# Storing the last 128 tokens of an attention and SwiGLU kernel in output order

## The chip, the cores and the metric

The kernel runs on one core of a Trainium2 chip. The metric is the time of one execution in device microseconds (us); lower is better. A core has five engines that run side by side and signal each other with semaphores: TensorE (PE: matmuls, with the loading of weights, PEld, beside them), VectorE (DVE), ScalarE (ACT), GpSimd (POOL) and SyncE (SP). Transfers between DRAM and the on-chip memory (SBUF) are issued by SP, ACT or POOL and carried out by 16 DMA engines. Matmuls write to PSUM, which has eight banks.

## The reference

Inputs are `q`, `k`, `v` of shape (8, 8, 576, 64), that is batch, head, token and head dimension, and three weight matrices. Linear attention gives 8 x 576 = 4608 rows of 512, and a SwiGLU block works on these:

```python
q_s = softmax(q, axis=-1)                 # over the head dimension
k_s = softmax(k, axis=2)                  # over the tokens
kv  = einsum('bhsd,bhse->bhde', k_s, v)
a   = einsum('bhsd,bhde->bhse', q_s, kv)
x   = a.transpose(0, 2, 1, 3).reshape(4608, 512)
g   = x @ w_gate                          # 512 -> 1536
out = (g * sigmoid(g) * (x @ w_val)) @ w_out   # 1536 -> 512, float32
```

## The kernel before

**Token order.** A batch has S = 576 tokens. Token number 9p + t of a batch (p from 0 to 63, t from 0 to 8; T = 9) is loaded so that a partition holds nine neighbouring tokens. In the transposed activations `xt` the column of that token is 576b + 64t + p. So 64 neighbouring columns are 64 tokens that lie nine rows apart in the output, and a block of 128 columns is two such groups, t and t + 1.

**Stages.** Attention of a batch (exponentials on ACT, sums and normalization on DVE, transposes, small matmuls) fills `xt`. The feed-forward part runs over chunks of columns: the first has 576, the second 448, and seven more have 512. The function `m_unit` (line 272) makes one of 12 slices of the hidden layer for a chunk: 4 matmuls for the gate and 4 for the value (line 284), a Silu on ACT (line 291) into `sg`, and one multiply on DVE (line 292) into `hr`. `hr` is a ring of 1536 columns. The function `o_unit` (line 320) then multiplies 128 columns of `hr`, as the stationary operand, with `wo` (12 matmuls, line 309), copies the 128 x 512 result to SBUF (line 110) and stores it with `store` (line 294). Because hidden columns become output partitions, the partition order of the result is the column order of `hr`. So `store` needs two transfers, each from 64 partitions to rows that lie nine apart.

**Order.** All instructions are written out by hand inside `tc.manual_schedule()`. The output blocks of one chunk are made among the units of the next (lines 524 to 547). In the last chunk (`final`, columns 4096 to 4607), units stand beside the output blocks 28 to 30; behind the units come block 31 (line 556), blocks 32 to 34 of the last chunk itself, and block 35 with `o_last` (line 323). `o_last` makes the 512 output columns in two pieces, 320 and 192, each with 12 matmuls (line 329), a copy (line 333) and a store of its own, so that the first piece is stored while the second is computed.

**Queues.** All output blocks but the last are stored by SP, two issues each. The last block's two pieces are stored by SP (lower 64 partitions) and ACT (upper 64). SP also issues the loads of `q`, `k`, `v` (line 77) and the DMA transposes (line 180), in program order. `load_kv(b)` (line 83) loads keys and values of batch b for both groups G of four heads; it is called for batches 4 to 7 in unit 8 of the chunk two batches earlier. The loads of the last batch are cut in two pieces (`BANKS`: t from 0 to 4, and 5 to 8), all but the values of G = 1. The transfers of SP and ACT take eight completion semaphores in turn, and a transfer waits until the one before it on the same semaphore has landed.

Of the kernel before, what the change touches and what calls it, by code (L numbers as in the profile page):

```python
# [15 lines left out]
def kernel(  # L16
# [10 lines left out]
    nc = tc.nc  # L27

    B, H, S, D = q.shape
    d_model, d_ff = moe_w_gate.shape  # L30
# [3 lines left out]
    T = S // 64  # L34
# [3 lines left out]
    BANKS = ((0, 5), (5, T))  # L38
# [8 lines left out]
    def bank(name):  # L47
        return psp.tile([128, 512], FP32, tag="ps", name=name)
# [5 lines left out]
    hr = const.tile([128, MT, RING], BF16, name="hr", tag="hr")  # L54
# [10 lines left out]
    def head_ap(src, b, G, t0=0, t1=T):  # L65
        return bass.AP(
            tensor=src.tensor,
            offset=src[b, 4 * G].offset + 64 * t0,
            ap=[[T * 64, 128], [2 * HSTR, 2], [1, (t1 - t0) * 64]],
        )  # L70

    def load(what, src, b, G, pieces=((0, T),), after=None):
        t_ = ld.tile([128, 2, T * 64], FP32, tag=what, name=what)
        raw[what, b, G] = t_
        last = None
        for t0, t1 in pieces:
            last = nc.sync.dma_start(out=t_[:, :, 64 * t0:64 * t1], in_=head_ap(src, b, G, t0, t1))  # L77
            if after is not None:
                tc.add_manual_dep(last.ins, after.ins.name, SYNC, reason="order of loads")
                after = None  # L80
        return last

    def load_kv(b):
        whole = ((0, T),)
        last = b == B - 1
        for G in range(NG):
            load("k", k, b, G, BANKS if last else whole)
            load("v", v, b, G, BANKS if last and G == 0 else whole)

    def w_slice(dst, src, c0, n):  # L90
        ap = bass.AP(
# [24 lines left out]
    def exp_of(what, b, G, pieces=((0, T),)):  # L116
        s = st.setdefault((b, G), {})
        e = s["e" + what] = at.tile([128, T, 2, 64], BF16, tag="e" + what, name="e" + what)
        src = raw[what, b, G].rearrange("p h (t d) -> p t h d", d=64)
        for t0, t1 in pieces:  # L120
            nc.scalar.activation(out=e[:, t0:t1], in_=src[:, t0:t1], func=AF.Exp)  # L121
# [21 lines left out]
    def norm_mul(b, G, pieces=((0, T),), engs=None):  # L143
        s = st[b, G]
        eq2 = s["eq"].rearrange("p t h d -> p (t h) d")
        qs = s["qs"] = at.tile([128, T, 128], BF16, tag="qs", name="qs")
        for (t0, t1), eng in zip(pieces, engs or (nc.vector, nc.vector)):
            n = 2 * (t1 - t0)
            last = eng.tensor_mul(  # L149
                qs[:, t0:t1, :].rearrange("p t (h d) -> p (t h) d", d=64),  # L150
                eq2[:, 2 * t0:2 * t1, :],
                s["rr"][:, 2 * t0:2 * t1].to_broadcast([128, n, 64]),
            )
        return last
# [22 lines left out]
    def turn_dma(b, G):  # L177
        s = st[b, G]
        qt = s["qt"] = at.tile([128, T, 128], BF16, tag="qt", name="qt")
        nc.sync.dma_start_transpose(out=qt, in_=s["qs"].rearrange("p t c -> p (t c)"))  # L180
# [38 lines left out]
    def kv_both(b):  # L219
        if ("kv", b) not in st:  # L220
            st["kv", b] = [bank("kv") for _ in range(2)]
        for G in range(NG):
            kv_mm(b, G, st["kv", b], 256 * G)

    def scale_both(b):
        kn = st["kn", b] = at.tile([128, 2, NG, 64], BF16, tag="kn2", name="kn2")
        for g in range(2):
            kv = st["kv", b][g].rearrange("p (G c) -> p G c", c=256)
            kvr = at.tile([128, NG], FP32, tag=f"kvrr{g}", name="kvr")
            nc.vector.reciprocal(out=kvr, in_=kv[:, :, 64])  # L230
            nc.vector.tensor_mul(kn[:, g], kv[:, :, 0:64], kvr.to_broadcast([128, NG, 64]))
# [37 lines left out]

    def m_unit(c0, n, m, by_group=False):
        ms = slice(m * 128, (m + 1) * 128)
        parts = [(c0, n)] if n <= 512 else [(c0, 320), (c0 + 320, n - 320)]
        gu = []
        for nm in ("g_ps", "u_ps"):
            ps = [bank(nm) for _ in parts]
            gu.append(ps)
        steps = [(a, kk, i) for a in range(2) for kk in range(KT) for i in range(len(parts))]
        if by_group:  # L280
            steps.sort(key=lambda a: (a[1] // 2, a[0], a[2], a[1]))
        for a, kk, i in steps:
            c, w_ = parts[i]
            nc.tensor.matmul(  # L284
                out=gu[a][i][:, 0:w_], lhsT=(wg, wv)[a][:, kk, ms], rhs=xt[:, kk, c:c + w_],
                start=(kk == 0), stop=(kk == KT - 1),
            )
        for g_ps, u_ps, (c, w_) in zip(gu[0], gu[1], parts):
            r = c % RING
            sg = ff.tile([128, 512], BF16, tag="sg", name="sg")  # L290
            nc.scalar.activation(out=sg[:, 0:w_], in_=g_ps[:, 0:w_], func=AF.Silu)  # L291
            nc.vector.tensor_mul(hr[:, m, r:r + w_], sg[:, 0:w_], u_ps[:, 0:w_])  # L292

    def store(j, o_sb, c0=0, c1=512, engs=(nc.sync, nc.sync)):
        for half in range(2):
            b, t = divmod(2 * j + half, T)
            dst = bass.AP(
                tensor=out.tensor,
                offset=out[b * S + t, c0].offset,
                ap=[[T * d_model, 64], [1, c1 - c0]],  # L300
            )
            engs[half].dma_start(out=dst, in_=o_sb[64 * half:64 * half + 64, c0:c1])

    def o_mm(j, o_ps=None, m0=0, m1=MT):
        if o_ps is None:
# [14 lines left out]
    def o_unit(j):  # L320
        o_out(j, o_mm(j))

    def o_last(j):
        r0 = (j * 128) % RING
        o_sb = osb.tile([128, 512], FP32, tag="o_sb", name="o_sb")
        for c0, n in ((0, 320), (320, 192)):
            o_ps = bank("o_ps")
            for m in range(MT):
                nc.tensor.matmul(  # L329
                    out=o_ps[:, 0:n], lhsT=hr[:, m, r0:r0 + 128], rhs=wo[:, m, c0:c0 + n],  # L330
                    start=(m == 0), stop=(m == MT - 1),
                )
            nc.vector.tensor_copy(out=o_sb[:, c0:c0 + n], in_=o_ps[:, 0:n])  # L333
            store(j, o_sb, c0, c0 + n, (nc.sync, nc.scalar))

# [1 line left out]
    with tc.manual_schedule():  # L339
# [113 lines left out]
        for m in range(MT):  # L453
            m_unit(0, S, m, by_group=(m == 0))
# [6 lines left out]
        p = [None, None]  # L461
# [43 lines left out]
        for ci, (c0, n) in enumerate(chunks):  # L505
            b = ci + 2
            jo = 4 * ci
            att = b < B
            more = b + 1 < B
            final = ci == len(chunks) - 1  # L510
            for m in range(MT):
                if ci == 0:
                    if m == 3:
                        norm_mul(b, 1)
                        turn_dma(b, 1)
                    elif m == 5:
                        kv_both(b)
                        scale_both(b)
                    elif m == 6:
                        exp_of("k", b + 1, 0)  # L520
                        exp_of("k", b + 1, 1)
                        cast_v(b + 1, 0)
                        cast_v(b + 1, 1)
                elif m == 3:
                    if att:
                        exp_of("q", b, 0)
                        exp_of("q", b, 1)
                        norm_sum(b, 0)
                    o_unit(jo)
                    if att:  # L530
                        norm_mul(b, 0)
                        turn_dma(b, 0)
                    o_unit(jo + 1)
                    if att:
                        norm_sum(b, 1)
                elif m == 4 and att:
                    norm_mul(b, 1)
                    turn_dma(b, 1)
                elif m == 7:
                    if more:  # L540
                        exp_of("k", b + 1, 0)
                        exp_of("k", b + 1, 1)
                        cast_v(b + 1, 0)
                        cast_v(b + 1, 1)
                    o_unit(jo + 2)
                    if not final:
                        o_unit(jo + 3)
                if m == 8 and more:
                    for G in range(NG):
                        load("q", q, b + 1, G)  # L550
                    if b + 2 < B:
                        load_kv(b + 2)
                m_unit(c0, n, m, by_group=(ci == 0 and m == 0))
                if att and m == (10 if ci == 0 else 9):
                    x_and_next_kv(b)
        o_unit(jo + 3)
        last = n_tok // 128 - 4
# [33 lines left out]
```

## Time and profile before

| what | value |
|---|---|
| median of 4 runs | 312.23 us (312.04 to 312.9) |
| the profiled execution's own time | 312.04 us |
| its span, first to last instruction | 309.8 us |
| granted TensorE clock | 0.998 of full |
| TensorE busy | 301.5 us, 97% of the span |
| DVE, ACT, POOL busy | 160.7, 146.2 and 32.8 us |
| last matmul of the last block ends, by the chain | 305.9 us |
| last copy to SBUF | 305.94 to 306.30 us |

A page gives the busy time of each engine and the chain of work that ended last, followed back from the last instruction. A row of a group has the line, the engine, the operation, output and input names, shapes and the count, then the busy time and the mean of one in ns, then the engine's idle time before these instructions and what ended it. Timeline rows begin with the start and the duration in us; "x2" merges neighbours. Issue rows have the count, the KB of one transfer and the us from issue to landing. SPq and ACTq are the queues of SP and ACT.

### The profile page before, as it was taken

How to read it: one execution, taken by the hardware profiler on the slowest of the kernel's cores; microseconds unless marked ns; L12 is line 12 of the kernel's file. 1: busy time of each engine (PE TensorE's matmuls, PEld its weight loads, DVE VectorE, ACT ScalarE, POOL GpSimd, SP SyncE). 2: the span in 40 equal slices, each digit the busy share in tenths (PEclk: the TensorE clock that was granted, in tenths of full speed). 3: DMA queues.
4: the chain of work that ended last, by engine and by line, in shares of the span. 5: the costliest groups of instructions: out<-in, count | busy, mean ns of one | idle time of the engine just before them, and what ended most of it. 6: DMA issues, size and time to landing. Idle time of an engine off the chain costs nothing.

```text
span 309.8 us, 5455 instructions
## 1 busy us (share of the span) xinstructions
PE 301.5 (97%) x2182; PEld 149.7 (48%) x2182; DVE 160.7 (52%) x274; ACT 146.2 (47%) x214; POOL 32.8 (11%) x39
## 2 busy tenths in 40 slices
PE   6799999999999999999999999999999999999995
PEld 2588745554444444454444444444444444444443
DVE  3844487945754566365826493539353324333321
ACT  5743578785674375447464737455043113312300
POOL 2960021510200110002000200000000000000000
PEclk9999999999999999999999999999999999999999
DMA  7999999999337815590739252505310302020034
GB/s 271 192 197 207 277 389 390 352 209 389 90 76 218 310 34 111 138 381 11 144 75 362 92 123 62 182 0 107 73 34 0 70 13 55 3 68 11 22 70 104
DMA packets 42506, 45.78 MB, mean 148 GB/s; under 512 B 19568, under 2 KB 27248, under 8 KB 42480
## 3 DMA queue, kind: packets, MB, share of 16 engines
q1 hardware_dynamic: 33568, 39.99, 43.3%
q0 software_dynamic: 8752, 5.31, 12.0%
q8 instruction: 17, 0.28, 0.3%
q10 hardware_dynamic: 160, 0.13, 0.2%
q14 instruction: 9, 0.07, 0.1%
HBM read 37.75 MB, written 9.44 MB: 152 GB/s over the span
## 4 chain that ended last, share of the span: by engine, by line
PE 94%; DMA 2%; DVE 1%; ACT 0%; SPq 0%; issue 0%
PE g_ps L284 30%; PE u_ps L284 30%; PE o_ps L309 29%; DMA q<-in_q_dram 2%; PE kv L189 2%; PE xp L245 1%; PE o_ps L329 1%; PE tp L164 0%; DVE qs L149 0%; DVE rs L135 0%; SPq L77 0%; PE xp L202 0%; ACT eq L121 0%; ACT xt L259 0%; DVE o_sb L333 0%
## 5 line engine op out<-in xcount | busy, mean ns | idle before, releaser
L291 ACT ACTIVATE sg<-g_ps 128x512 bf16<-128x512 f32 (+2 forms) x120 | 64.6, 554 | 133.6 <-PE g_ps L284 131.8
L292 DVE TENSOR_TENSOR hr<-sg,u_ps 128x512 bf16<-128x512 bf16 (+2 forms) x120 | 74.2, 630 | 87.3 <-PE u_ps L284 81.6
L284 PE MATMUL g_ps<-xt,wg 128*128 128x512 bf16 (+2 forms) x480 | 111.4, 358 | 0.1
L284 PE MATMUL u_ps<-xt,wv 128*128 128x512 bf16 (+2 forms) x480 | 111.3, 358 | 0.0
L309 PE MATMUL o_ps<-wo,hr 128*128 128x512 bf16 x420 | 93.9, 379 | 0.0
L284 PEld LDWEIGHTS <-wv 128*128 128x128 bf16 x480 | 47.0, 98 | 46.4
L284 PEld LDWEIGHTS <-wg 128*128 128x128 bf16 x480 | 46.3, 98 | 45.5 <-issue 0.6
L309 PEld LDWEIGHTS <-hr 128*128 128x128 bf16 x420 | 40.9, 98 | 48.6
L110 DVE COPY o_sb<-o_ps 128x512 f32<-128x512 f32 x33 | 22.5, 680 | 39.2 <-PE o_ps L309 39.2
L124 POOL CAST vb<-v 128x1152 bf16<-128x1152 f32 x14 | 17.9, 1281 | 136.1 <-DMA v<-in_v_dram 128.6
L135 DVE TENSOR_REDUCE rs<-eq 128x18 f32<-128x1152 bf16 (+2 forms) x18 | 21.7, 1214 | 13.1 <-ACT eq L121 13.1
L149 DVE TENSOR_TENSOR qs<-eq,rr 128x1152 bf16<-128x1152 bf16 (+2 forms) x18 | 21.7, 1216 | 0.1
L121 ACT ACTIVATE eq<-q 128x1152 bf16<-128x1152 f32 (+2 forms) x18 | 18.3, 1051 | 4.3 <-DMA q<-in_q_dram 4.2
L121 ACT ACTIVATE ek<-k 128x1152 bf16<-128x1152 f32 (+2 forms) x17 | 17.9, 1101 | 0.5 <-DMA k<-in_k_dram 0.5
L291 ACT ACT_TABLE_LOAD x12 | 15.4, 1283 | 0.2
L121 ACT ACT_TABLE_LOAD x11 | 14.1, 1283 | 0.2
L259 ACT CAST xt<-xp 128x512 bf16<-128x512 f32 x14 | 7.8, 586 | 4.4 <-PE xp L245 4.4
L260 DVE CAST xt<-xp 128x512 bf16<-128x512 f32 x14 | 9.0, 682 | 0.7 <-PE xp L245 0.7
L374 PE MATMUL idle<-zero 128*128 128x512 bf16 x20 | 6.5, 479 | 2.7 <-DVE rs L135 1.5
L189 PEld LDWEIGHTS <-ek 64*64 64x64 bf16 x504 | 6.3, 107 | 1.7 <-ACT ek L121 0.4
L189 PE MATMUL kv<-vb,ek 64*64 64x65 bf16 x504 | 6.7, 194 | 0.0
L245 PE MATMUL xp<-qt,kn 64*64 64x512 bf16 (+1 forms) x112 | 6.7, 292 | 0.0
(43 smaller groups left out, 62.7 us busy)
## 6 DMA issues: line engine op xcount, KB each, us to landing
q<-in_q_dram SPq DMA_DIRECT2D x16, 576.0 KB, 5.0
out_dram<-o_sb SPq DMA_DIRECT2D x70, 128.0 KB, 2.3
k<-in_k_dram SPq DMA_DIRECT2D x13, 576.0 KB, 7.6
v<-in_v_dram SPq DMA_DIRECT2D x13, 576.0 KB, 8.7
wo<-in_moe_w_out_dram POOLq DMA_DIRECT2D x4, 384.0 KB, 15.4
k<-in_k_dram SPq DMA_DIRECT2D x3, 320.0 KB, 7.7
k<-in_k_dram SPq DMA_DIRECT2D x3, 256.0 KB, 7.9
wg<-in_moe_w_gate_dram POOLq DMA_DIRECT2D x1, 512.0 KB, 11.0
```

The costliest lines, as they stand in the source:

```text
L110: eng.tensor_copy(out=out, in_=in_)
L121: nc.scalar.activation(out=e[:, t0:t1], in_=src[:, t0:t1], func=AF.Exp)
L124: return nc.gpsimd.tensor_copy(out=vbs[G][:, :, :, 0:64], in_=raw["v", b, G].rearrange("p h (t d) -> p t h d", d=64),)
L135: i = nc.vector.reduce_sum(out=rs[:, 2 * t0:2 * t1], in_=eq2[:, 2 * t0:2 * t1, :], axis=mybir.AxisListType.X)
L149: last = eng.tensor_mul(qs[:, t0:t1, :].rearrange("p t (h d) -> p (t h) d", d=64), eq2[:, 2 * t0:2 * t1, :], s["rr"][:, 2 * t0:2 * t1].to_ ...
L189: nc.tensor.matmul(out=kv[g][HALF[h], c:c + 65], lhsT=ek[HALF[g], t, h, :], rhs=vbs[G][HALF[g], t, h, :], start=(t == 0), stop=(t == T - 1),)
L245: nc.tensor.matmul(out=o[h][HALF[g], c:c + 64 * (t1 - t0)], lhsT=kn[HALF[h], g, G, :], rhs=qt[G][HALF[h], t0:t1, 64 * g:64 * g + 64], star ...
L260: nc.vector.tensor_copy(out=xt[:, 2 * G + 1, c0:c0 + 512], in_=main[G][1])
L284: nc.tensor.matmul(out=gu[a][i][:, 0:w_], lhsT=(wg, wv)[a][:, kk, ms], rhs=xt[:, kk, c:c + w_], start=(kk == 0), stop=(kk == KT - 1),)
L291: nc.scalar.activation(out=sg[:, 0:w_], in_=g_ps[:, 0:w_], func=AF.Silu)
L292: nc.vector.tensor_mul(hr[:, m, r:r + w_], sg[:, 0:w_], u_ps[:, 0:w_])
L309: nc.tensor.matmul(out=o_ps, lhsT=hr[:, m, r0:r0 + 128], rhs=wo[:, m, :], start=(m == 0), stop=(m == MT - 1),)
```

## The change

In the last chunk the multiply into `hr` is made in two: 384 columns as before, and the last 128 with a permuted write, so that the two tokens of a pair (t = 7 and t = 8 for the same p, neighbouring rows of the output) become neighbouring columns. The output partitions of block 35 are then in the order of the output's rows. `o_last` stores each column piece by one transfer over 64 pairs of rows, the 320 columns from ACT and the 192 from SP, instead of two transfers over 64 rows each. `store` loses its column and queue arguments. In `load_kv`, two more loads are cut in two pieces: the keys of G = 1 of batch 6 (B - 2) and the values of G = 1 of batch 7, so the number of transfers from SP and ACT together stays the same.

```diff
-            load("k", k, b, G, BANKS if last else whole)
-            load("v", v, b, G, BANKS if last and G == 0 else whole)
+            load("k", k, b, G, BANKS if last or (b == B - 2 and G == 1) else whole)
+            load("v", v, b, G, BANKS if last else whole)
...
-    def m_unit(c0, n, m, by_group=False):
+    def m_unit(c0, n, m, by_group=False, final=False):
...
-            nc.vector.tensor_mul(hr[:, m, r:r + w_], sg[:, 0:w_], u_ps[:, 0:w_])
+            w1 = w_ - 128 if final else w_
+            nc.vector.tensor_mul(hr[:, m, r:r + w1], sg[:, 0:w1], u_ps[:, 0:w1])
+            if final:
+                nc.vector.tensor_mul(
+                    hr[:, m, r + w1:r + w_].rearrange("k (p h) -> k h p", h=2),
+                    sg[:, w1:w_].rearrange("k (h p) -> k h p", h=2),
+                    u_ps[:, w1:w_].rearrange("k (h p) -> k h p", h=2),
+                )
...
     def o_last(j):
         r0 = (j * 128) % RING
         o_sb = osb.tile([128, 512], FP32, tag="o_sb", name="o_sb")
-        for c0, n in ((0, 320), (320, 192)):
+        b, t = divmod(2 * j, T)
+        for c0, n, eng in ((0, 320, nc.scalar), (320, 192, nc.sync)):
...
             nc.vector.tensor_copy(out=o_sb[:, c0:c0 + n], in_=o_ps[:, 0:n])
-            store(j, o_sb, c0, c0 + n, (nc.sync, nc.scalar))
+            dst = bass.AP(
+                tensor=out.tensor,
+                offset=out[b * S + t, c0].offset,
+                ap=[[T * d_model, 64], [d_model, 2], [1, n]],
+            )
+            eng.dma_start(out=dst, in_=o_sb[:, c0:c0 + n])
...
-                m_unit(c0, n, m, by_group=(ci == 0 and m == 0))
+                m_unit(c0, n, m, by_group=(ci == 0 and m == 0), final=final)
```

More of the change, by code (lines that the diff above doesn't have):

```diff
@@ L291, in m_unit, with store @@
             nc.scalar.activation(out=sg[:, 0:w_], in_=g_ps[:, 0:w_], func=AF.Silu)
-            nc.vector.tensor_mul(hr[:, m, r:r + w_], sg[:, 0:w_], u_ps[:, 0:w_])
-    def store(j, o_sb, c0=0, c1=512, engs=(nc.sync, nc.sync)):
+            w1 = w_ - 128 if final else w_
[6 more added lines that the diff above has]
+                )
+    def store(j, o_sb):
         for half in range(2):
@@ L298, in store @@
                 tensor=out.tensor,
-                offset=out[b * S + t, c0].offset,
-                ap=[[T * d_model, 64], [1, c1 - c0]],
+                offset=out[b * S + t, 0].offset,
+                ap=[[T * d_model, 64], [1, d_model]],
             )
-            engs[half].dma_start(out=dst, in_=o_sb[64 * half:64 * half + 64, c0:c1])
+            nc.sync.dma_start(out=dst, in_=o_sb[64 * half:64 * half + 64, :])
     def o_mm(j, o_ps=None, m0=0, m1=MT):
```

## The prediction

> **What bounds the kernel now.** I read the page first (busy shares and chain), then the chain in the last microseconds, then the issue rows of the stores in the same stretch, and last the neighbours that the change touches.
>
> The page says that TensorE is the bound:
>
> ```profile
> span 309.8 us, 5455 instructions
> PE 301.5 (97%) x2182; PEld 149.7 (48%) x2182; DVE 160.7 (52%) x274; ACT 146.2 (47%) x214; POOL 32.8 (11%) x39
> ...
> PE 94%; DMA 2%; DVE 1%; ACT 0%; SPq 0%; issue 0%
> ```
>
> What has to be seen is that DVE and ACT are half idle and not on the chain. Work added to them costs time only where it makes TensorE wait, or where it lies behind the last matmul.
>
> The chain of the last 10 us, and the stores that follow it (timeline of the issuing queues, then the issues of the stretch 306.3 to 309 with the KB of each and the us to landing):
>
> ```profile
> 299.82 3.45 PE o_ps L309 x16
> 303.28 2.63 PE o_ps L329 x24
> 305.91 0.02 issue
> 305.94 0.36 DVE o_sb L333
> ```
>
> ```profile
> 306.33 0.53 ACTq L302 DMA_DIRECT2D out_dram<-o_sb  x1
> ...
> 306.35 0.47 SPq L302 DMA_DIRECT2D out_dram<-o_sb  x1
> ```
>
> ```profile
> out_dram<-o_sb ACTq DMA_DIRECT2D x1, 48.0 KB, 2.5
> out_dram<-o_sb SPq DMA_DIRECT2D x1, 48.0 KB, 2.3
> ```
>
> The last copy ends at 305.94 + 0.36 = 306.30. ACT's half lands at 306.33 + 2.5 = 308.8, SP's at 306.35 + 2.3 = 308.6. ACT's lands last. From there to 309.8 run the closing waits and the barrier (line 586), 1.0 us that the change leaves as they are. So only the stretch 306.3 to 308.8 can get shorter; everything before is TensorE at one matmul per 0.216 us (10.36 us for 48 in the chain's row at 292.92).
>
> **The change part by part.**
>
> *Two more load pieces on SP (load_kv).* Batch 6 gets one more K issue and batch 7 one more V issue. A piece's issue takes 0.42 to 0.54 us on SP. SP is then idle for long:
>
> ```profile
> 165.43 0.42 SPq L77 DMA_DIRECT2D v<-in_v_dram  x1
> 178.75 1.12 SPq L302 DMA_DIRECT2D out_dram<-o_sb  x2
> ```
>
> After batch 7's loads it is free from 165.85 to 178.75, and after batch 6's from 132.08 to 146.27. What is queued behind, stores and transposes, starts no later. Every DMA from there on takes the next completion semaphore of eight, so a load may wait for one issued eight earlier: the tenth load of batch 7 would wait for the second, issued at about 161.6 and landed within 5 us. If SP stood until 166.6, the gap is still 12 us. Readers: batch 7's V is read by the cast on POOL at 174.32, whose result the matmuls of line 189 take at 196.86; batch 6's K is read by ACT at 154.93 while its loads were issued at about 131 with 8.5 us to landing. Margins of 14 us and more against shifts of about 0.5: zero. If that cover were gone, each piece would cost its 0.5 us.
>
> *Twelve DVE multiplies become 24 (last chunk).* One 128x512 multiply takes 0.69 us here. The 384-wide one lies between the rows for 320 (488 ns) and 512 (684 ns): 0.55. The 128-wide one has its nearest row in the 128x128 multiply of line 231 (292 ns); its stride-two write is in no row, and its upper bound is four times its columns, 0.69. Sum 0.84, at most 1.24, against 0.69. TensorE gives one unit every 8 x 0.216 = 1.73 us, and DVE waits for it:
>
> ```profile
> 291.30 0.69 DVE L292 TENSOR_TENSOR hr<-sg,u_ps 128x512 bf16<-128x512 bf16 x1 [1.04 <-PE u_ps L284]
> 293.03 0.69 DVE L292 TENSOR_TENSOR hr<-sg,u_ps 128x512 bf16<-128x512 bf16 x1 [1.04 <-PE u_ps L284]
> ```
>
> The 1.04 us of idle time takes the extra 0.15 (at most 0.55). The last pair ends at 293.03 + 0.84 = 293.9 (at most 294.3). Block 32 reads its first part from 295.35, after block 31's 12 matmuls, and the permuted columns are read from 303.1. Zero; without block 31 as cover it would be the 0.15. The PSUM banks come free 0.15 to 0.55 us later, but each is reused only eight tiles later, some 7 us.
>
> *Waits.* In the built program TensorE has the same instructions in the same order. Because a PSUM bank or an `sg` buffer now has two readers, a dozen matmul groups of the last chunk take one more wait (the weight load on DVE, the matmul on TensorE's own write of that bank some 40 matmuls, 9 us, earlier), and nine Silus of ACT one on ACT itself. All are met long before. Before has waits on weight loads and on matmuls too, and keeps 0.216 us through them: zero. Upper end: were each an instruction of its own that can't be hidden, at the 51 ns of a TensorE semaphore wait (line 586), 12 x 51 = +0.6 us.
>
> *The last block's stores.* Four transfers over 64 rows become two over 128: 320 columns (160 KB) from ACT, 192 columns (96 KB) from SP. The copy in front of them is unchanged, so SP issues at 306.35 as now, with an idle queue. No row has a 128-row store. The nearest rows are SP's 64-row stores: 80 KB lands in 2.0, 128 KB alone in 2.2 (the block of 296.3). 96 KB lies between: 2.1, landing at 308.45 instead of 308.8: -0.35. The shorter end is 2.0: -0.45. The longer end is that the transfer behaves as two halves one after the other: SP's 128 KB stores follow each other by 0.52, and the second lands 2.3 after its own issue, 2.8 in all, 309.15: +0.35. I take -0.35, nearer the rows by size, because both halves flow at once today and SP's row is the shorter one at both pairs (2.0 against ACT's 2.4 at 80 KB, 2.3 against 2.5 at 48 KB).
>
> ACT's 320-column transfer is issued at 305.47. With ACT's 2.4 for half of it, and 2.8 + 0.4 at the long end, it lands between 307.9 and 308.7. It ends the kernel only at its long end and would then leave -0.1.
>
> A rule that speaks against the gain: the Trainium skill, "DMA: Bandwidth & Descriptors", section "Issuing engines are not separate DMA queues", says that transfers from SP and ACT run on the same engines and that the issuer saves only its own issue time. The rows above show ACT's landing 0.2 to 0.4 us after SP's at equal size. [...]
>
> *Sum.* 0 + 0 + 0 - 0.35. The profiled execution took 312.04 (span 309.8, 2.2 outside it), so 311.7 for its like. It is 0.19 below the median of the four runs, 312.23; on that median the forecast is 311.9, -0.1%. A measurement of this kernel can tell about 0.2%, 0.62 us, from no change, so this counts as no change.
>
> **The rivals.**
>
> *No gain at all (chance 0.13).* Landing goes by size or by the slowest row, not by the queue, and 96 KB on SP lands as late as ACT's 48 KB now, or ACT's 160 KB takes its place as the last. For it: the halves differ by only 0.2 us, and SP's 48 KB took longer (2.3) than its 80 KB (2.0), so bytes do not order them alone. Time 312.1 to 312.6; call it 312.3.
>
> *Slower: the paired pattern runs on fewer DMA engines (0.06).* The DRAM side now counts 64 pairs of 2 rows, the SBUF side 128 partitions. From 80 to 128 KB a store gains 0.2 to 0.3 us for 3 KB more per engine (48 KB over 16), about 0.08 us per KB. On 8 engines the 96 KB are 6 KB more for each: 2.6, 308.95, +0.15. On 4 they are 18 KB more: 3.5, 309.9, +1.0, so 313.3. It decides (over 0.62) where the landing passes 3.1, at five engines or fewer. Against it: the loads, whose patterns have 3 dimensions on both sides, show 369 to 438 GB/s over whole slices, so three dimensions as such do not narrow a transfer. The skill's page, section "Why a DMA increments its semaphore by 16 and not by 1", takes the largest count up to 16 that divides both slowest dimensions, 64 and 128, hence 16; no run here shows that for the paired pattern yet.
>
> *Slower: the extra waits break TensorE's stream in the last chunk (0.07).* At 12 x 51 ns it is +0.6, less the -0.35 of the tail: 312.2 to 312.5, up to 312.9 if the tail gives nothing. For it: weight load and matmul of one pair have not both waited in before's last stretch. Against it: the gapless 0.216 us.
>
> *The change does what it says* is not in doubt in the program (one transfer per column piece); that the tail is hidden anyway is excluded, since nothing else ends after 306.3.
>
> **How the numbers follow.** My case, the tail shorter by 0.1 to 0.45 and the rest hidden, has 0.74; its own range is 311.6 to 312.2, and 0.16 of the 0.74 falls below 311.6, because the medians of a few runs spread as the four here do (312.04 to 312.9). No gain: 0.13 (0.01 of it faster by chance, 0.12 same). Fewer engines: 0.06 slower. Waits: 0.07 (0.03 same, 0.04 slower). That gives faster 0.17, same 0.73, slower 0.10. The range, 311.3 to 312.7, takes in the best tail with scatter at one end, and a tail longer by 0.35 or half the waits at the other; fewer engines stay outside.
>
> **What would show it.** In the profile after: PE at about 301.5 us busy and the last matmul group ending at 305.9; 12 multiplies of about 0.55 and 12 of about 0.29 with DVE still idle before them; one ACT issue at 305.47 (160 KB) and one SP issue at 306.35 (96 KB) with 2.1 us to landing; a span of about 309.4. A landing of 2.5 or more says that size decides; over 3 that engines are missing. Gaps in the rows of line 284 in the last chunk, or a last copy later than 305.94, say that the waits or DVE were not hidden. A 128-wide multiply above 1.17 us (1.73 - 0.55) would overrun the unit and prove the DVE step wrong.

## The result and the profile after

| | before | after |
|---|---|---|
| median | 312.15 us (62 executions, 311.68 to 313.1) | 311.66 us (38 executions, 311.13 to 312.86) |
| ratio | | 0.9985, 95% interval 0.998 to 0.9991 |
| profiled execution, its span | 312.04, 309.8 | 311.6, 309.8 |

By the ratio the change makes the kernel 0.47 us faster (0.28 to 0.62 by the interval). That is less than the 0.2% of the prediction's bound, but more than nothing. The page of the changed kernel, busy shares and then the engines on the chain:

```profile
span 309.8 us, 5467 instructions
PE 302.8 (98%) x2182; PEld 150.4 (49%) x2182; DVE 161.7 (52%) x286; ACT 146.2 (47%) x214; POOL 32.9 (11%) x39
...
PE 96%; DMA 1%; DVE 0%; ACT 0%; issue 0%
```

TensorE bounds it as before. The extra 1.3 us of busy TensorE are the idle matmuls of the warm-up at the start (7.9 us of them instead of 6.5), not the feed-forward part. The chain at the end (start, duration, what), then the queues' rows of the last transfer, then its landing:

```profile
299.93 3.45 PE o_ps L317 x16
303.38 2.63 PE o_ps L338 x24
306.01 0.02 issue
306.04 0.36 DVE o_sb L342
```

```profile
306.42 0.61 SPq L348 DMA_DIRECT2D out_dram<-o_sb  x1
```

```profile
out_dram<-o_sb SPq DMA_DIRECT2D x1, 96.0 KB, 2.0
```

The chain has the same shape and lengths, 0.10 us later, and this shift is there already at the first feed-forward matmul. The last landing comes 2.08 us after the last copy; before, it came 2.51 us after it.

**Yet the two spans are equal.** Two profiled executions 0.44 us apart in their own time have spans of 309.8 us each. So the end of the program has to be taken in three parts: last copy to last landing, last landing to the end of the span, and the time outside the span (own time less span). The first two come from the trace's records of engines and semaphores. A transfer leaves sixteen landing records there, and "landing" is the last of them:

| us | copy to landing | landing to end of span | outside the span | sum |
|---|---|---|---|---|
| before | 2.51 | 0.97 | 2.27 | 5.75 |
| before, second execution | 2.55 | 0.99 | 2.29 | 5.83 |
| after | 2.08 | 1.30 | 1.83 | 5.21 |

The sum is 0.5 to 0.6 us shorter, which is the measured gain. The first column gives 0.43 to 0.47 and the other two together about 0.1. They also shift against each other, by +0.3 and -0.4 us, which hides the gain from the span.

**The multiplies and the loads.** DVE's groups in the last chunk of the changed kernel (busy us, mean ns, then DVE's idle time before them):

```profile
L293 DVE TENSOR_TENSOR hr<-sg,u_ps 128x384 bf16<-128x384 bf16 x12 | 6.7, 554 | 11.9 <-PE u_ps L284 11.9
L296 DVE TENSOR_TENSOR hr<-sg,u_ps 128x128 bf16<-128x128 bf16 x12 | 3.5, 294 | 0.0
```

The pair takes 0.85 us. The permuted write costs next to nothing: a plain multiply of the same 128 columns takes 280 ns in the kernel "Only the second multiply" below. DVE still waits 0.99 us for TensorE before each pair. SP issues batch 7's last two load pieces and then the next stores:

```profile
165.50 1.52 SPq L77 DMA_DIRECT2D v<-in_v_dram  x2
178.85 1.12 SPq L310 DMA_DIRECT2D out_dram<-o_sb  x2
```

SP is idle for 11.8 us between them, and the stores come at 178.85, the same 0.10 later as everything else.

### The profile page after: what moved, and what is told of

Read it like the earlier page. It is cut to its first block, busy times and chain, and to the rows that moved or that the text cites. A ratio compares the mean times of both kernels' runs of the same rounds, so it can differ in the third digit from the quotient of the medians.

```text
span 309.8 us, 5467 instructions
## 1 busy us (share of the span) xinstructions
PE 302.8 (98%) x2182; PEld 150.4 (49%) x2182; DVE 161.7 (52%) x286; ACT 146.2 (47%) x214; POOL 32.9 (11%) x39
## 4 chain that ended last, share of the span: by engine, by line
PE 96%; DMA 1%; DVE 0%; ACT 0%; issue 0%
PE g_ps L284 30%; PE u_ps L284 30%; PE o_ps L317 29%; PE kv L189 2%; PE xp L245 1%; PE idle L388 1%; DMA q<-in_q_dram 1%; PE tp L164 1%; PE o_ps L338 1%; DVE rs L135 0%; PE xp L202 0%; PE kv L411 0%; ACT eq L121 0%; ACT xt L259 0%; PE ks L397 0%; DVE o_sb L342 0%
## 5 line engine op out<-in xcount | busy, mean ns | idle before, releaser
L293 DVE TENSOR_TENSOR hr<-sg,u_ps 128x512 bf16<-128x512 bf16 (+3 forms) x120 | 72.6, 617 | 86.5 <-PE u_ps L284 80.7
L388 PE MATMUL idle<-zero 128*128 128x512 bf16 x20 | 7.9, 561 | 2.7 <-DVE rs L135 1.5
```

The costliest lines, as they stand in the source:

```text
L293: nc.vector.tensor_mul(hr[:, m, r:r + w1], sg[:, 0:w1], u_ps[:, 0:w1])
L388: i = nc.tensor.matmul(out=idle, lhsT=zero[:, 0:128], rhs=zero, start=True, stop=True)
```

## The experiments

Three explanations stood at the start. Theory A says that the issuing queue of the last transfer counts. Theory B says that one transfer in place of two counts. Theory C says that the gain comes from somewhere else than the tail. As results came, theories D, E and P were added. They concern code fetches: single packets of 8 KB on the queue that the profile calls "instruction", by which an engine's program is taken to be loaded piece by piece. Single times scatter by several tenths of a us, and 10 to 12 executions give intervals of 0.2 to 0.4% of full width. So the verdicts on tenths rest on the traces, and the times only bound them.

### The queues exchanged

```diff
-        for c0, n, eng in ((0, 320, nc.scalar), (320, 192, nc.sync)):
+        for c0, n, eng in ((0, 320, nc.sync), (320, 192, nc.scalar)):
```

> Only the queues of the two merged transfers of the last block are exchanged: 320 columns from SP, 192 columns from ACT. Theory A (the issuer counts: a store from ACT lands about 0.3 us later than one from SP): the last transfer lands about 2.35 us after its issue instead of 2.05, the time is about 311.9 us, ratio to before 0.999. Theory B (one transfer in place of two is what counts, the queue is worth nothing): landing stays at about 2.05, time 311.7, ratio 0.9985. Theory C (the gain is not made in the tail): 311.7 as well, whatever the landing.

Measured: median 311.63, ratio 0.9984 (0.9965 to 1.0004). The last transfer, from ACT:

```profile
out_dram<-o_sb ACTq DMA_DIRECT2D x1, 96.0 KB, 2.1
```

It lands 2.14 us after the last copy, against 2.08 from SP. For this transfer the queue is worth 0.06 us, not 0.3. Theory A falls, and with it the reason that the prediction gave for its number.

### The permuted order with the old stores

```diff
-            dst = bass.AP(
-                tensor=out.tensor,
-                offset=out[b * S + t, c0].offset,
-                ap=[[T * d_model, 64], [d_model, 2], [1, n]],
-            )
-            eng.dma_start(out=dst, in_=o_sb[:, c0:c0 + n])
+            store(j, o_sb, c0, c0 + n, (nc.sync, nc.scalar))
...
```

> The changed kernel with the stores of before (four transfers over 64 rows, lower half from SP, upper half from ACT); the permuted multiply and the extra load pieces stay. The rows of block 35 then go to each other's places in the output. Theory A and B (the gain lies in the last transfers): 312.15 us, ratio 1.000, ACT's half landing about 2.4 us after its issue. Theory C (the gain comes from the load pieces, the shifted semaphores or the multiplies): 311.7 to 311.9. If the added multiplies and waits cost something that the tail hid: above 312.3.

Measured: median 312.1, ratio 0.9995 (0.9976 to 1.0013). By the time alone the gain is gone. The trace says otherwise. The old stores, four over 64 rows, land much sooner than in the kernel before:

```profile
out_dram<-o_sb SPq DMA_DIRECT2D x1, 48.0 KB, 1.9
out_dram<-o_sb ACTq DMA_DIRECT2D x1, 48.0 KB, 2.1
```

Last copy to last landing is 2.17, not 2.51. So 0.34 us of the tail has nothing to do with the stores' form. The sum of the three parts is 5.70 all the same, because landing to end of span took 1.69. This kernel has two transfers more than the others, so the last landing comes on the semaphore of the second of SP's nine closing waits; in the changed kernel it comes on that of the ninth. When it lands, seven more waits are still to be done. That cost 0.4 us and spoils this kernel as a control of the time.

### Without the extra load pieces

```diff
-            load("k", k, b, G, BANKS if last or (b == B - 2 and G == 1) else whole)
-            load("v", v, b, G, BANKS if last else whole)
+            load("k", k, b, G, BANKS if last else whole)
+            load("v", v, b, G, BANKS if last and G == 0 else whole)
```

> The changed kernel without the two extra load pieces. Theory A and B: 311.7 us, ratio 0.9985, the same tail (SP's 96 KB landing about 2.05 us after issue). Theory C, load pieces: 311.9 to 312.15. The transfers then end on other completion semaphores, so that the closing waits of SP may come in another order, worth at most 0.1 us.

Measured: median 311.96, ratio 0.9992 (0.9975 to 1.0009). The parts are 2.07, 1.03 and 2.30, in sum 5.40, between before (5.75) and after (5.21). The transfer lands as in the changed kernel; what is missing is 0.2 us behind the landing. That much is left of theory C. SP's program is two instructions shorter than in the changed kernel, and the 8 KB packet runs at 307.90, just behind the transfer's last packet.

### Only the last piece as one transfer

```diff
         for c0, n, eng in ((0, 320, nc.scalar), (320, 192, nc.sync)):
...
+            if c0 == 0:
+                store(j, o_sb, c0, c0 + n, (nc.sync, nc.scalar))
+                continue
...
```

> The changed kernel, but the 320-column piece is stored in two halves from SP and ACT as before (its rows go to each other's places in the output); only the 192-column piece is one transfer from SP. If the last transfer alone carries the gain (theories A and B): 311.7 us, ratio 0.9985, landing about 2.05 us after issue. If the first piece's halves get in its way on SP or in the DMA engines: landing 2.2 to 2.4, time 311.9 to 312.1.

Measured: median 311.98, ratio 0.9989 (0.9974 to 1.0005). The last piece lands 2.05 us after its issue and 2.07 after the copy, so the first piece's form does not matter to it. Landing to end of span is 1.68 here too, with one transfer more than the others: the closing waits again.

### The kernel before, once more

> The kernel before once more, for a second look at its tail. In the first profile one landing of each of the last two stores came 0.33 us behind the other fifteen (last landing 2.51 us after the last copy), while an 8 KB instruction transfer ran at 307.46 to 307.76, between their packets. Theory D (a code fetch of DVE at a fixed place of its program sits on one DMA engine and holds up the last stores): again about 2.5 us from last copy to last landing. If it was an accident of one execution: about 2.17 us, as with the same stores in e3_order_only.

No edit. One execution, 312.12 us. The stretch 307.3 to 308.3 by DMA queue (packets, MB, share of 16 engines):

```profile
q10 hardware_dynamic: 87, 0.05, 20.6%
q1 hardware_dynamic: 80, 0.05, 20.4%
q14 instruction: 1, 0.01, 3.2%
```

The single packet of the instruction queue is one of 8 KB. It ran at 307.33 for 0.51 us, among the packets of ACT (q10) and SP (q1). Of the sixteen landing records fifteen had come by 2.16 us after ACT's issue and 1.95 after SP's; the sixteenth came at 2.52 and 2.30. The first profile shows the same (2.16 and 2.47, 1.92 and 2.27), so this is no accident of one execution. In the changed kernel the same stretch has no such packet:

```profile
q1 hardware_dynamic: 144, 0.10, 30.8%
q10 hardware_dynamic: 35, 0.02, 7.5%
```

Its 8 KB came at 306.53, before the last transfer's packets.

### Only the second multiply

```diff
...
-            nc.vector.tensor_mul(hr[:, m, r:r + w_], sg[:, 0:w_], u_ps[:, 0:w_])
+            w1 = w_ - 128 if final else w_
+            nc.vector.tensor_mul(hr[:, m, r:r + w1], sg[:, 0:w1], u_ps[:, 0:w1])
+            if final:
+                nc.vector.tensor_mul(hr[:, m, r + w1:r + w_], sg[:, w1:w_], u_ps[:, w1:w_])
...
```

> The kernel before with one edit: the last chunk's multiply is made in two, 384 and 128 columns, in the old order. Stores and loads are those of before. DVE's program gets 12 instructions longer and so passes its 8 KB boundary about 10 us earlier. Theory D: no instruction transfer among the last stores, last copy to last landing about 2.17 us instead of 2.51, time 311.8, ratio 0.999. Theories A and B (the stores' form or queue is what counts): tail and time as before, 312.15, ratio 1.000.

Measured: median 312.09, ratio 1.0 (0.9978 to 1.0022). The 8 KB packet taken for DVE's moved from 304.82 to 296.68, yet another fetch still ran at 307.06, and the last landing came 2.46 us after the copy:

```profile
out_dram<-o_sb ACTq DMA_DIRECT2D x1, 48.0 KB, 2.4
out_dram<-o_sb SPq DMA_DIRECT2D x1, 48.0 KB, 2.2
```

Theory D falls: the fetch in the tail is not DVE's.

### One permuted multiply instead of two

```diff
-            w1 = w_ - 128 if final else w_
-            nc.vector.tensor_mul(hr[:, m, r:r + w1], sg[:, 0:w1], u_ps[:, 0:w1])
             if final:
...
                 nc.vector.tensor_mul(
-                    hr[:, m, r + w1:r + w_].rearrange("k (p h) -> k h p", h=2),
-                    sg[:, w1:w_].rearrange("k (h p) -> k h p", h=2),
-                    u_ps[:, w1:w_].rearrange("k (h p) -> k h p", h=2),
+                    hr[:, m, r:r + w_].rearrange("k (b p h) -> k b h p", h=2, p=64),
+                    sg[:, 0:w_].rearrange("k (b h p) -> k b h p", h=2, p=64),
+                    u_ps[:, 0:w_].rearrange("k (b h p) -> k b h p", h=2, p=64),
                 )
+            else:
+                nc.vector.tensor_mul(hr[:, m, r:r + w_], sg[:, 0:w_], u_ps[:, 0:w_])
```

> The changed kernel, but the last chunk's multiply stays one instruction that permutes all four blocks of 128 columns (so the rows of blocks 32 to 34 go to each other's places in the output). DVE's program is then as long as before. Theory D: DVE's code fetch comes back to about 1.5 us after the last copy begins, among the packets of SP's last transfer, which lands about 0.3 us later than in the changed kernel (2.3 to 2.4 us after the last copy instead of 2.08), time 311.9 to 312.0. Theories A and B: 2.08 us and 311.7, as the changed kernel. If a permuted multiply of 512 columns is slower than 0.69 us, its row shows it; up to 1.7 us it stays hidden.

Measured: median 311.82, ratio 0.9987 (0.9974 to 1.0). The three parts are 2.08, 1.30 and 1.84, those of the changed kernel. This is the second fall of theory D, and further evidence that DVE's work has no part in the result.

### Both halves of a piece on one queue

```diff
-        for c0, n in ((0, 320), (320, 192)):
+        for c0, n, eng in ((0, 320, nc.scalar), (320, 192, nc.sync)):
...
-            store(j, o_sb, c0, c0 + n, (nc.sync, nc.scalar))
+            store(j, o_sb, c0, c0 + n, (eng, eng))
```

> The kernel before, but both halves of the 192-column piece go through SP one after the other, both halves of the 320-column piece through ACT. The prediction's long end for one transfer over 128 rows was this price: the second half issued 0.52 us after the first and landing 2.3 us later, 2.8 us after the last copy, against 2.05 measured for the one transfer. If the queue takes the two halves without loss, landing at 2.2 to 2.4.

Measured: one execution, 312.13 us. SP's second half is issued 0.51 us after the first and lands 2.24 later, 2.77 after the copy, as the prediction's long end had it (2.8). The 8 KB packet starts at 308.47, just behind the last packet of the stores, and no landing record is late. One transfer over 128 rows is thus 0.7 us better than two in series, and only 0.07 better than two side by side.

### Eight more load pieces in the kernel before

```diff
-            load("k", k, b, G, BANKS if last else whole)
+            load("k", k, b, G, BANKS if b >= B - 2 else whole)
...
-                        load("q", q, b + 1, G)
+                        load("q", q, b + 1, G, BANKS if b >= 4 else ((0, T),))
```

> The kernel before with eight more load pieces (queries of batches 5, 6 and 7, keys of batch 6), so that the last transfers keep their semaphores and queues while SP's program gets longer in front of them. Theory E (the 8 KB code fetch that ran between the packets of the last stores is SP's own, and its place goes by the length of SP's program): no fetch between 306.5 and 308.5, no landing far behind its fifteen fellows, last copy to last landing 2.15 to 2.2 us instead of 2.5, time 311.8. Theories A and B (the form or the queue of the last stores makes the whole gain): 2.5 us and 312.15, as before. If load pieces cost time of their own: above 312.3.

This is the deciding run. Multiplies, stores, queues and semaphores of the last block are those of before. Longer in front of them are SP's program (230 recorded instructions instead of 222) and ACT's, which waits for the pieces (352 instead of 344). The stretch 306.9 to 307.9, in which the last stores' packets ran, by queue; then the stretch 300.5 to 301.5; then the stores:

```profile
q10 hardware_dynamic: 83, 0.05, 21.3%
q1 hardware_dynamic: 80, 0.05, 20.1%
```

```profile
q1 hardware_dynamic: 45, 0.06, 26.4%
q14 instruction: 1, 0.01, 1.9%
```

```profile
out_dram<-o_sb SPq DMA_DIRECT2D x1, 48.0 KB, 1.9
out_dram<-o_sb ACTq DMA_DIRECT2D x1, 48.0 KB, 2.1
```

The fetch has moved to 300.80, no landing record is late, and copy to landing is 2.15 us instead of 2.51 and 2.55. The other two parts are those of before (0.96 and 2.28), in sum 5.39. That the fetch is SP's and not ACT's shows in where it starts. In all 14 profiles it comes 1.05 to 1.79 us after SP begins its 207th recorded instruction, at 305.98 in the kernel before and at 299.56 here; ACT begins nothing here between 298.06 and 305.02. Theory E holds for the tail.

The times do not show it: median 312.14, ratio 1.0002 (0.9988 to 1.0016). The interval just reaches the 0.36 us that are expected. The lowest quarter of its 12 executions ends at 311.65 against 311.99 for the kernel before beside it, the highest quarter begins at 312.87 against 312.31. In the profiled execution (311.24) nothing was lost on the way: from the first gate matmul to the start of the last matmul it took 291.43 us, as before. Why more of its executions were late stays open.

### One piece of V for one of K

```diff
-            load("k", k, b, G, BANKS if last else whole)
-            load("v", v, b, G, BANKS if last and G == 0 else whole)
+            load("k", k, b, G, BANKS if last and G == 0 else whole)
+            load("v", v, b, G, BANKS if last else whole)
```

> The kernel before, but of batch 7 the values of G = 1 are loaded in two pieces and the keys of G = 1 whole: as many transfers as before, and one more wait on POOL, whose program has 70 instructions as in the changed kernel and not 69. Theory P (POOL's own code fetch at the end of its program then falls inside the closing barrier and not behind it): 0.35 to 0.45 us more between two of POOL's closing waits, 1.86 us outside the span instead of 2.29, and together 3.13 us from last landing to the end instead of 3.25; the time falls by 0.1 to 312.05. If the 1.86 us come from the stores: 2.29 as before. The last stores and SP's fetch stay, so the last landing stays 2.5 us after the last copy.

Measured: median 312.09, ratio 0.9999 (0.9987 to 1.0011). POOL's closing instructions, before and then here (duration min/median/max, first and last start):

```profile
L586 POOLq EVENT_SEMAPHORE  x4: 17/17/17, 309.0 to 309.7; - x4
L586 POOLq DRAIN  x3: 45/93/2803, 174.3 to 309.5; - x3
```

```profile
L586 POOLq EVENT_SEMAPHORE  x4: 17/17/17, 309.9 to 310.9; - x4
L586 POOLq DRAIN  x3: 45/93/2805, 174.9 to 310.3; - x3
```

From POOL's last drain to its last semaphore instruction it takes 0.17 us before and 0.53 here: 0.44 between the last two of its semaphore instructions instead of 0.08. The time outside the span is 1.79 to 1.89 us in all 12 executions. It is 2.23 to 2.36 in the kernel before, and 1.8 to 1.9 in the changed kernel. One more POOL instruction (69 recorded instead of 68) goes with it, without any edit of the stores. The same holds in the other runs: with 68 the profiles have 2.27 to 2.30 outside the span, with 69 they have 1.83 to 1.86. The parts are 2.53, 1.33 and 1.83: landing to the very end 3.16 instead of 3.24 to 3.28. Theory P holds for the exchange, and the net gain of about 0.1 is in the trace but within the noise of the times. That the 0.4 us are a fetch of POOL's code is not shown: the trace has no instruction packet between those two instructions (310.42 to 310.87).

### Six permuted multiplies

```diff
-                nc.vector.tensor_mul(
...
+                for _ in range(6):
+                    nc.vector.tensor_mul(
...
```

> The changed kernel with the permuted 128-column multiply made six times over in each of the last 12 units, 0.55 + 6 x 0.29 = 2.3 us of DVE per unit against 1.73 of TensorE. The prediction's bound (a unit is overrun above 1.73): TensorE waits, up to 12 x 0.57 = 6.8 us, 313 to 318. Rival: three output blocks of 2.59 us among the units, block 31 behind them and PSUM tiles that are taken again only after eight take up the excess, DVE falls at most about 5 us behind and no matmul waits: 311.7.

Measured: median 311.65, ratio 0.9987 (0.9975 to 0.9998), as the changed kernel. The stretch 262 to 306:

```profile
L297 DVE TENSOR_TENSOR hr<-sg,u_ps 128x128 bf16<-128x128 bf16 x72 | 21.5, 299 | 2.1
L318 PE MATMUL o_ps<-wo,hr 128*128 128x512 bf16 x84 | 18.6, 379 | 0.0
L284 PE MATMUL u_ps<-xt,wv 128*128 128x512 bf16 x60 | 15.4, 379 | 0.0
...
L291 ACT ACTIVATE sg<-g_ps 128x512 bf16<-128x512 f32 x15 | 9.0, 597 | 24.8 <-PE g_ps L284 21.4 <-DVE hr L297 3.4
```

DVE had 0.55 + 6 x 0.30 = 2.3 us of work per unit of 1.73. ACT waited 3.4 us in all for DVE to free its `sg` buffers, and TensorE had no idle time. This profiled execution took 313.34 us, but the loss lies in its start: its matmuls run 1.76 us behind those of the changed kernel from 27.2 us on, and stay at 1.76 to the last. The rival expectation holds.

### A shared last copy

```diff
-            nc.vector.tensor_copy(out=o_sb[:, c0:c0 + n], in_=o_ps[:, 0:n])
+            cut = n if c0 == 0 else 96
+            nc.vector.tensor_copy(out=o_sb[:, c0:c0 + cut], in_=o_ps[:, 0:cut])
+            if cut < n:
+                nc.scalar.copy(out=o_sb[:, c0 + cut:c0 + n], in_=o_ps[:, cut:n])
```

> A try at a faster kernel: the changed kernel with the last copy (128x192) shared, 96 columns by DVE and 96 by ACT. The copy takes 0.36 us; halves should take 0.25 to 0.28 each side by side, the last store is issued about 0.1 us earlier, 311.55. If both engines' reads of one PSUM bank run one after the other, or ACT starts later than DVE: no gain, 311.7.

Measured: median 311.96, ratio 0.9995 (0.9985 to 1.0005). It is no faster than the changed kernel. The timeline shows why:

```profile
306.23 0.65 ACTq L351 DMA_DIRECT2D out_dram<-o_sb  x1
306.70 0.26 DVE L343 COPY o_sb<-o_ps 128x96 f32<-128x96 f32 x1 [0.50 <-PE o_ps L338]
307.14 0.24 ACT L345 COPY o_sb<-o_ps 128x96 f32<-128x96 f32 x1 [13.63 <-DMA out_dram<-o_sb]
307.40 0.61 SPq L351 DMA_DIRECT2D out_dram<-o_sb  x1
```

The halves take 0.26 and 0.24 as hoped, but ACT issues the first piece's store until 306.88 and then goes through waits on older stores, and starts 0.44 after DVE. With the first piece's store issued by SP it might pay; that was not run.

## Why the prediction was right, and where only its number was

**The sum.** Forecast was -0.35 us and 311.9, no change by the bound of 0.2%; measured -0.47 and 311.66. The time lies in the range, and within 0.2% of the kernel before, as forecast. That the -0.35 came so near is luck: the transfer's own duration was sized rightly, but most of what it gains on the one before has a cause that the prediction did not have.

**Loads.** Right as to transfers: SP idle for 11.8 us behind them, nothing late. What the step did not see: each piece also lengthens programs. POOL got one more wait, and SP two more issues.

**Multiplies and waits.** Right: 0.85 us per pair against 0.84, and the 48 matmuls behind the units take 10.36 us in the chain as before. One bound was wrong: "above 1.17 us (1.73 - 0.55) would overrun the unit and prove the DVE step wrong". Six multiplies overran the unit by 0.6 us and no matmul waited. The bound compared DVE with TensorE unit by unit. That the three output blocks among the units and the free PSUM tiles carry the backlog was expected before that run and fits it; no run takes them away.

**The stores.** The size was right: 2.1 us to landing forecast, 2.05 measured. The reason was wrong. The step read ACT's 2.5 and SP's 2.3 as what these queues cost ("SP's row is the shorter one at both pairs"). The runs show a part of 0.34 to 0.40 us, the tail's difference to kernels with the same stores (2.15 and 2.17 against 2.51 and 2.55), that goes with one late landing record beside an 8 KB code fetch. A sign of it stood in the prediction's rows: SP's 48 KB took longer (2.3) than its 80 KB (2.0). Without the fetch, in the kernel with eight more pieces, the 48 KB take 1.86 from SP and 2.12 from ACT. So the fetch made both halves late, and ACT's half takes 0.21 to 0.26 longer than SP's with or without it. But that is so of two halves issued side by side: a transfer that runs last by itself lands only 0.06 later from ACT. One transfer instead of two side by side is worth about nothing beyond that (2.14 from ACT against 2.15 for the old form).

The fetch follows a place in SP's program. In the changed kernel SP reaches its 207th instruction, the wait ahead of its last store, at 305.29 instead of 305.98, because it issues none of the first piece. The fetch starts at 306.53, ahead of the last packets (307.69 to 308.13). No run puts it between the packets of the one merged transfer, so what it would cost there is not shown.

So the rule of the Trainium skill ("DMA: Bandwidth & Descriptors", "Issuing engines are not separate DMA queues"), which the prediction set behind its rows, was nearer to the truth for the last transfer than its reading of the rows: 0.06 us lie between the two kernels that differ only in the exchanged queues.

**The closing part.** The step "1.0 us that the change leaves as they are" failed: 0.97 became 1.30, and the time outside the span fell from 2.27 to 1.83. So the span of about 309.4, which the prediction named as a sign, did not come; it stayed at 309.8.

**The rivals.** "No gain at all" is refuted by the ratio's interval, though its thought that the landing does not go by the queue was nearly right (0.06). "Fewer engines" is refuted by 2.05 us. "The waits break TensorE's stream" is refuted by the chain. None of them named code fetches.

| part of the gain | us | from |
|---|---|---|
| fetch out of the last packets | 0.36 to 0.40 | before against eight load pieces: 2.51 and 2.55 to 2.15 |
| queue and form of the last transfer | 0.07 | 2.15 to 2.08 |
| landing to the very end | 0.11 to 0.15 | 3.24 and 3.28 to 3.13 |

Together they make 0.54 to 0.62, where the times say 0.28 to 0.62. The first row rests on traces, mostly one for each kernel; the times of the kernel with eight more pieces do not confirm it.

## What to carry to other kernels

When only a tail can change, split it at the last copy, the last landing, the end of the span and the end of the execution; a span alone can stay equal while the time falls. Before a landing time in a profile is called the cost of a transfer or of its queue, look for a third transfer between the packets, the instruction queue's included. Adding a few instructions to an engine's program, or one transfer to the count, shifted parts of the tail here by 0.3 to 0.4 us, so compare versions with the same number of transfers.

## What the runs showed of the hardware

- One 8 KB instruction packet (0.31 to 0.52 us in these runs) among the packets of a store went with one of sixteen landing records being 0.26 to 0.37 us late, in four profiles of four where it ran beside the packets of both last stores (before twice, the second multiply, the V piece). In the other ten profiles it ran ahead of the packets of the last piece or just behind them, and no landing of that piece came more than 0.06 us behind the one before it.
- The order of the closing waits matters: where the last transfer ended on a semaphore that SP waits for early, landing to end of span took 1.68 and 1.69 us instead of 1.30.
- Executions differ at the start: the first gate matmul came between 13.64 and 15.04 us in the profiles here. That alone is 1.4 us, three times the effect of this change, and the profile with six multiplies loses another 1.5 us between there and 27.2 us.
- The permuted store is issued in 0.61 us on SP, where one over 64 rows took 0.47; with the queue idle it cost nothing that the landing shows.
